# Grouping the softmax-maximum and value matmuls of two attention steps

## The chip, the core and the metric

The kernel runs on one core of a Trainium2 chip. A core has a matrix engine (TensorE: PE in the profile, its weight loads PEld), VectorE (DVE), ScalarE (ACT), GpSimd (POOL) and SyncE (SP, which here only issues DMAs). Each engine works through its own queue of instructions, and semaphores tie the queues together. The results of TensorE land in PSUM, which this kernel treats as eight banks of 128x512 f32 values; VectorE and ScalarE read them from there. The metric is device time of one execution in microseconds, lower being better.

## The reference, cut to what matters

Two times over, an attention block and a gated block are applied to `x` (2048 tokens, width 448), with the same weights in both rounds:

```python
x = x + attention(layernorm(x))      # 16 query heads of 28, one shared key and value head
x = x + glu(layernorm(x))            # (sigmoid(x Wg) * (x Wu)) Wd, inner width 1792
# attention:
scores = einsum("bhqd,bkd->bhqk", q, k) * Dh ** -0.5
o = einsum("bhqk,bkd->bhqd", softmax(scores), v)      # then @ wo
```

The softmax needs the maximum of each query's scores over all 2048 keys before the exponentials can be formed.

## The kernel before, in words

**Tiles.** A layer (l = 0, 1) is one attention block and one gated block. The 2048 queries are cut into 16 units of 128 (u = 0..15), the keys into 16 tiles of 128 (kt = 0..15), and the 16 heads into 4 groups of 4, so that one matmul has 4 heads x 128 queries = 512 columns. One step is one pair (u, kt), and a layer has 256 steps.

**What a step issues** is written out as a string, `ORDER = "FSFSFSFSPXM"` (L901), read letter by letter in the loop at L922:

- `S`, four times: `scores` (L507). One matmul (L510, tile `s`, a PSUM bank) and the exponential on ScalarE (L513), which writes the probabilities `P` in f32, from a pool of 8 tiles.
- `P`: `pv` (L516), the values of the *previous* step. Four products 128x512, each of them two matmuls, in four column strips of 32 (L521, tile `pv`, a PSUM bank of its own for the whole unit). At the end of a unit ScalarE copies them out (L525, `pvs`).
- `M`: one turn of the generator `mx_gen` (L464), which works for the *next* unit. A turn is four matmuls in four row strips of 32 (L480, tile `mx`, four banks) of one group of heads with 512 keys, and four VectorE reductions of a whole bank each (L484, `mp`). Sixteen turns make a unit. Then two small VectorE operations give the maxima `m16` (L493, L494), and `fin` (L496) transposes them on TensorE (L499, `mt`), copies them out (L501, `mr`) and sends them by a DMA from GpSimd's queue (L502) into row 28 of the query tile `QS`, from which `scores` of that unit subtracts them. `fin` waits in the list `late` for `LT = 1` turns. In unit 0 two steps take an extra turn (`MORE`), so the maxima run three turns ahead of the units.
- `X`: `tick` (L536) starts what is due of the units already finished: dividing by the sums, the output projection (`fc`, L606, twelve matmuls `wo` in one go), layer norm, transposes by DMA, and in layer 0 the keys and values of the next layer (`kv`). It also sets `rate`, the nanoseconds of filler per step: what is left, divided by the steps to go.
- `F`, four times: `Filler.slice` (L767). It first calls `flush`, which issues the deferred evictions that are due, and then lets the filler generators issue matmuls up to a quarter of `rate`, by costs written into the kernel (110 ns for a matmul of 256 columns, 190 for 448). What `tick` issued counts as debt: slices issue nothing until it is paid.

**The filler** is mostly the gated block of two finished units (`bulk`, L651): for each of 7 pairs of inner tiles a chain of 22 matmuls into `gp`, another into `up` (L345), the tanh on ScalarE (L665), the product on VectorE (L673, which frees `up`), and `parts`: a ScalarE scaling (L676) two slices after that and a VectorE remainder (L677) one slice later, into a tile `h` (pool of 10, `HB`). Then 2 x 42 matmuls `dn` (L702). The pool of `h` also holds the first tiles of `x` at the start (`load_x0`, L792). In each layer the first block of filler of this kind appears when unit 3 begins; before that the filler is query projections (`qp`).

**Banks.** One bank is kept for `pv`. The other seven are one pool, from which `s`, `mx`, `gp`, `up`, `dn`, `wo` and all other results take theirs in the written order; a matmul that has been given a bank waits until its last reader is done.

Of the kernel before, what the change touches and what calls it, by code (L numbers as in the profile page):

```python
# [19 lines left out]
def interleaved_layers_kernel(ctx: ExitStack, tc: tile.TileContext, x, wq, wk, wv, wo, wg, wu, wd, out, layers=2):  # L20
# [9 lines left out]
    H, Dh = 16, 28  # L30
    NT, NB, G, KT, FC = S // 128, S // 512, H // 4, S // 128, F // 128
    U = NT
    TB, WB, HB = 2, 4, 10
    NBL = NT // TB
    EPS = 1e-5

# [29 lines left out]
    def defer(fn, lag=0):  # L66

        pend.append((now[0] + lag, fn))
# [87 lines left out]
    def prep_q():  # L156
        parts = wk1.tile([128, 4], F32, name="parts", bufs=1)
        for c in range(4):
            junk = wk1.tile([128, D], F32, tag="P", name="junq", bufs=8)
            squares(parts[:, c:c + 1], rq[:, c], junk)  # L160
        nc.vector.tensor_reduce(mxa[:, 2:3], parts, axis=AX.X, op=OP.add)
        nc.vector.memset(WQ[:, :, :, :, Dh:32], 0.0)
        yield
        yield from scales(mxa[:, 2:3], 1, pwa[:, 2:3], swa[:, 2:3])
        for c in range(4):
            r = rq[:, c].rearrange("p (h d) -> p h d", d=Dh)
            split(WQ[:, 0, c, :, 0:Dh], WQ[:, 1, c, :, 0:Dh], r, swa[:, 2:3])
            yield
        nc.vector.tensor_scalar(esc, pwa[:, 2:3], pwa[:, 0:1], None, op0=OP.mult)
        nc.vector.tensor_scalar(esc, esc, Dh ** -0.5 * 2.0 ** -14, None, op0=OP.mult)  # L170
# [258 lines left out]
    QS, QH, PVS = {}, {}, {}  # L429
    late = []  # L430
    stored = set()
    LT = 1

    def load_qs(l, u):
        b, t = divmod(u, 4)
# [28 lines left out]
    def mx_gen(l):  # L464

        load_qh(l, 0)
        for u in range(U):
            qh = QH[l, u]
            mp = wk1.tile([128, 4, 4, NB], F32, name="mp", bufs=2)
            for kb in range(NB):  # L470
                for g in range(G):
                    for i in range(len(late) - 1, -1, -1):
                        late[i][0] -= 1
                        if late[i][0] <= 0:
                            late.pop(i)[1]()
                    assert KVD[l] >= 4 * (kb + 1)
                    ps = [psf.tile([128, 512], F32, tag=BANKS["m"], name="mx", bufs=NBK[BANKS["m"]])
                          for _ in range(4)]
                    for h in range(4):
                        nc.tensor.matmul(ps[h], qh[32 * h:32 * h + 32, g],  # L480
                                         KK[l][32 * h:32 * h + 32, 1, kb * 512:(kb + 1) * 512], start=True,
                                         stop=True, tile_position=(32 * h, 0))
                    for h in range(4):
                        nc.vector.tensor_reduce(mp[:, g, h, kb:kb + 1], ps[h], axis=AX.X, op=OP.max)  # L484
                    ps = None
                    if kb == NB - 1 and g == 2 and u + 1 < U:
                        load_qh(l, u + 1)
                    if kb * 4 + g == 7:
                        load_qs(l, u)
                    yield  # L490
            m32 = wk1.tile([128, 16], F32, name="m32")
            m16 = wk1.tile([128, 16], F16, name="m16")
            nc.vector.tensor_reduce(m32, mp.rearrange("p g h k -> p (g h) k"), axis=AX.X, op=OP.max)  # L493
            nc.vector.tensor_scalar(m16, m32, -(2.0 ** -15), None, op0=OP.mult)  # L494

            def fin(u=u, m16=m16):  # L496
                stored.add(("m", l, u))
                p = fps([16, 128], F16, "mt")
                nc.tensor.transpose(p, m16, id16)  # L499
                r = wk1.tile([16, 128], F16, name="mr")  # L500
                nc.vector.tensor_copy(r, p)  # L501
                nc.gpsimd.dma_start(QS[l, u][28:29].rearrange("o g h n -> o (g h) n"), r)  # L502
            late.append([LT, fin])
        while late:
            late.pop(0)[1]()

    def scores(l, u, kt, g, P):  # L507
        assert ("m", l, u) in stored, (l, u, kt)
        s = psf.tile([128, 512], F32, tag=BANKS["s"], name="s", bufs=NBK[BANKS["s"]])
        nc.tensor.matmul(s, KK[l][0:96, 0, kt * 128:(kt + 1) * 128], QS[l, u][:, g].rearrange("p h n -> p (h n)"),  # L510
                         start=True, stop=True)
        p = wk1.tile([128, 512], F32, tag="P", name="P", bufs=8)
        nc.scalar.activation(p, s, AF.Exp, scale=esc)  # L513
        P.append(p)

# [32 lines left out]
    class Block:  # L548
# [8 lines left out]
        def tile(self, u):  # L557
# [39 lines left out]
                yield  # L597

            def fb():
                oT = v["oT"] = wk1.tile([128, 2, 512], F16, name="oT")  # L600
                nc.scalar.copy(oT[:, 0], v["lb"])
                defer(lambda: nc.vector.tensor_tensor(oT[:, 1], v["lb"], oT[:, 0], op=OP.subtract))  # L602
                return
                yield
# [46 lines left out]
        def bulk(self):  # L651
            l, b, XT2 = self.l, self.b, self.XT2
            hs = []

            def glu(f):

                for j in range(2):
                    if f + j + 2 < FC:
                        self.load_w(f + j + 2)
                w = [self.wt.pop(f + j) for j in range(2)]  # L660
                gp = fps([128, 2, TB * 128], F32, "gp")
                for j in range(2):
                    yield from chain(gp[:, j], lambda a, c, k: w[j][:k, 0, a, c], lambda c, k: XT2[:k, c], C256, True)
                th = wk1.tile([128, 512], F32, tag="s2", name="th", bufs=3)
                defer(lambda: nc.scalar.activation(th, gp.rearrange("p j n -> p (j n)"), AF.Tanh, scale=gsc))  # L665
                up = fps([128, 2, TB * 128], F32, "up")
                for j in range(2):
                    yield from chain(up[:, j], lambda a, c, k: w[j][:k, 1, a, c], lambda c, k: XT2[:k, c], C256, True)
                h = wk1.tile([128, 2, 512], F16, name="h", bufs=HB)

                def ev():
                    t = th
                    nc.vector.scalar_tensor_tensor(t, th, 1.0, up.rearrange("p j n -> p (j n)"), op0=OP.add, op1=OP.mult)  # L673

                    def parts():
                        nc.scalar.activation(h[:, 0], t, AF.Copy, scale=2.0 ** -17)  # L676
                        defer(lambda: nc.vector.scalar_tensor_tensor(h[:, 1], t, 2.0 ** -17, h[:, 0], op0=OP.mult,  # L677
                                                                     op1=OP.subtract), 1)
                    defer(parts, 2)
                defer(ev)  # L680
                hs.append(h)

            for f in range(0, FC, 2):
                yield from glu(f)

            if not self.last and b % 2 == 0:
                XTQ[l + 1, b // 2] = big.tile([128, 7, 512], F16, tag="big", name="XT1")
            need(2 + FC)
            for t in range(TB):
                yield from self.down(t, hs)  # L690
# [207 lines left out]
        nmx += 1  # L898

    early[0] = False  # L900
    ORDER = "FSFSFSFSPXM"  # L901
    MORE = (5, 10)
    FIRST = KT * TB + 16
    KEEP = 28000
# [1 line left out]
    for l in range(layers):  # L906
# [10 lines left out]
        while late:  # L917
            late.pop(0)[1]()
        fill.slice(QCH)
        prevP = None  # L920
        rate = 0.0
        for step in range(U * KT):  # L922
            u, kt = divmod(step, KT)
            P = []
            for o in ORDER:
                if o == "S":
                    scores(l, u, kt, len(P), P)
                elif o == "M":
                    for _ in range(1 + (u == 0 and kt in MORE)):
                        next(mx, None)  # L930
                elif o == "P":
                    if prevP is not None:
                        pv(*prevP)
                elif o == "X":
                    if u and kt == 1:
                        b = (u - 1) // TB
                        if (l, b) not in BLK:
                            BLK[l, b] = Block(l, b)
                        later(*BLK[l, b].tile(u - 1))
                    if l == 0:  # L940
                        paced(step)
                    tick()
                    fed = sum(BLK[l, b].fed == TB for b in range(NBL) if (l, b) in BLK)
                    if fed < NBL - 1:
                        rate = fill.left / max(FIRST + TB * KT * fed - step, 1)
                    else:
                        rate = max(fill.left - KEEP, 0) / (U * KT - step)
                else:
                    fill.slice(rate / ORDER.count("F"))
            prevP = (l, u, kt, P)  # L950
        pv(*prevP)
        flush(True)
        later(*BLK[l, NBL - 1].tile(U - 1))
        if not final:
# [33 lines left out]
```

## Time and profile before

| | us |
|---|---|
| median of 3 runs | 2358.56 (2357.25 to 2362.03) |
| the profiled execution: its own time | 2358.22 |
| its span on the core | 2356.4 |
| TensorE busy | 2239.1 |
| VectorE busy | 1635.5 |
| ScalarE busy | 1559.2 |
| GpSimd busy | 336.8 |

The clock granted to TensorE was 0.985 of full speed over the span. Busy time of TensorE is that of matmul records whose ends are modelled, so the start of one matmul to the start of the next says more than the duration. In a row of the timeline, a figure in brackets is the idle time of that engine before the instruction, and behind it stands what ended it. "DVE L484 ... x4" is a run of four such instructions in a row, merged. A row of a waits view gives the waiting group, what released it, the sum in microseconds, the number of times and the longest one.

### The profile page before, as it was taken

Reading aid. Unit: us, or ns where it says so; the run is one execution under the profiler, and the core shown is the slowest. Engines: PE = TensorE matmul, PEld = TensorE weight load, DVE = VectorE, ACT = ScalarE, POOL = GpSimd, SP = SyncE. Lnnn points to the kernel's source line nnn. Section 1 sums busy time; section 2 is a strip of 40 time slices with the busy share of each in tenths; the row PEclk is TensorE's granted clock in tenths of the full one; section 3 lists DMA queues with packets and bytes.
Section 4 is the critical chain, followed back from the end, with each engine's and each line's share of the span. In section 5 each row is a group of like instructions: output and inputs, shape, how many; then the busy total and the mean of one; then the engine's idle time right before and its main releaser. Section 6 shows DMA issues by size and latency. Waiting matters only on the chain.

```text
span 2356.4 us, 41206 instructions
## 1 busy us (share of the span) xinstructions
PE 2239.1 (95%) x15736; PEld 1003.2 (43%) x15736; DVE 1635.5 (69%) x2917; ACT 1559.2 (66%) x2598; POOL 336.8 (14%) x602
## 2 busy tenths in 40 slices
PE   5888899999999999999998989999999999999999
PEld 3322243444444444444572224444444444444456
DVE  6888787777777777773358877867676777777321
ACT  5588676776667677677413777767676776767751
POOL 5203763100110110001101011000000000000010
PEclk9799999999999999999998999999999999999999
DMA  3244652323313132333342112222231313223133
GB/s 114 65 126 124 201 190 81 90 73 98 96 58 109 58 93 70 94 92 78 96 139 53 27 49 92 87 78 83 62 103 58 98 55 101 76 82 94 57 111 119
DMA packets 208071, 213.88 MB, mean 91 GB/s; under 512 B 139952, under 2 KB 168304, under 8 KB 207872
## 3 DMA queue, kind: packets, MB, share of 16 engines
q1 hardware_dynamic: 202496, 196.36, 28.5%
q0 software_dynamic: 5376, 14.87, 1.8%
q8 instruction: 123, 2.02, 0.4%
q14 instruction: 76, 0.62, 0.1%
HBM read 175.37 MB, written 23.59 MB: 84 GB/s over the span
## 4 chain that ended last, share of the span: by engine, by line
PE 51%; DVE 5%; DMA 1%; ACT 1%; issue 0%; SPq 0%; POOL 0%; ACTq 0%; DVEq 0%; POOLq 0%
PE pv L521 12%; PE s L510 10%; PE dn L702 8%; PE gp L345 7%; PE up L345 7%; DVE mp L484 4%; PE mx L480 4%; PE wo L612 2%; PE qp L345 1%; ACT P L513 0%; DMA sums<-rc 0%; DMA KK<-ktl 0%; DMA rc<-sums 0%; DMA sums<-pvs 0%; DVE st L297 0%
## 5 line engine op out<-in xcount | busy, mean ns | idle before, releaser
L513 ACT ACTIVATE P<-s,esc 128x512 f32<-128x512 f32 x2048 | 1307.8, 690 | 509.2 <-PE s L510 492.1
L484 DVE TENSOR_REDUCE mp<-mx 128x1 f32<-128x512 f32 x2048 | 1267.2, 681 | 412.2 <-PE mx L480 408.1
L510 PE MATMUL s<-QS,KK 96*128 96x512 f16 x2048 | 761.1, 381 | 52.7 <-DVE mp L484 34.8
L345 PEld LDWEIGHTS <-wgu 128*128 128x128 f16 x4928 | 458.6, 98 | 241.3 <-issue 94.5
L521 PE MATMUL pv<-P,VV 128*32 128x512 f32 x4096 | 547.3, 607 | 0.0
L345 PE MATMUL up<-XT,wgu 128*128 128x256 f16 x2464 | 375.6, 272 | 0.8 <-DVE mp L484 0.8
L345 PE MATMUL gp<-XT,wgu 128*128 128x256 f16 x2464 | 375.2, 274 | 0.2
L702 PE MATMUL dn<-WD,h 128*128 128x448 f16 x1344 | 321.7, 352 | 0.0
L510 PEld LDWEIGHTS <-KK 96*128 96x128 f16 x2048 | 194.5, 97 | 172.1 <-issue 93.0
L480 PE MATMUL mx<-KK,QH 32*128 32x512 f16 x2048 | 223.2, 392 | 20.7 <-ACT QH L402 4.8
L480 PEld LDWEIGHTS <-QH 32*128 32x128 f16 x2048 | 53.5, 91 | 396.5 <-issue 378.1
L702 PEld LDWEIGHTS <-h 128*128 128x128 f16 x1344 | 124.1, 98 | 136.6 <-issue 22.6
L521 PEld LDWEIGHTS pv<-P,VV 128*32 128x32 f32 x4096 | 80.9, 108 | 204.4 <-issue 192.6
L595 POOL TENSOR_TENSOR lb<-pvs,lb 128x512 f32<-128x512 f32 x32 | 40.5, 1265 | 800.3 <-DMA lb<-sums 679.4
L676 ACT ACTIVATE h<-th 128x512 f16<-128x512 f32 x112 | 70.2, 627 | 86.4 <-DVE th L673 86.3
L345 PE MATMUL qp<-XT,WQ 128*128 128x512 f16 x352 | 114.5, 403 | 3.8 <-DVE mp L484 2.4
L673 DVE SCALAR_TENSOR_TENSOR th<-th,up 128x512 f32<-128x512 f32 x112 | 75.8, 677 | 59.0 <-PE up L345 46.5
L303 POOL TENSOR_SCALAR rs<-mv 128x1 f32<-128x1 f32 (+2 forms) x53 | 13.6, 256 | 686.4 <-DVE mv L298 682.9
L677 DVE SCALAR_TENSOR_TENSOR h<-th,h 128x512 f16<-128x512 f32 x112 | 77.7, 693 | 46.7 <-ACT h L676 46.7
L665 ACT ACTIVATE th<-gp,gsc 128x512 f32<-128x512 f32 x112 | 76.8, 685 | 47.7 <-PE gp L345 47.7
L612 PE MATMUL wo<-WO,oT 128*128 128x448 f16 x384 | 78.4, 353 | 0.3 <-DVE oT L602 0.2
L345 PEld LDWEIGHTS <-WQ 128*128 128x128 f16 x352 | 34.2, 101 | 64.2 <-issue 41.1
(126 smaller groups left out, 834.3 us busy)
## 6 DMA issues: line engine op xcount, KB each, us to landing
wgu<-wgu_d SPq DMA_DIRECT2D x224, 512.0 KB
QS<-qd SPq DMA_DIRECT2D x384, 32.0 KB
lb<-sums SPq DMA_DIRECT2D x128, 64.0 KB
xr<-in_A_x_dram SPq DMA_DIRECT2D x32, 224.0 KB
qd<-qst POOLq DMA_DIRECT2D x28, 256.0 KB, 2.7
wgu_d<-sgu POOLq DMA_DIRECT2D x14, 512.0 KB, 3.8
QH<-qd SPq DMA_DIRECT2D x28, 128.0 KB
x2d<-x SPq DMA_DIRECT2D x16, 224.0 KB
```

The lines of the kernel that those rows point to most:

```text
L345: nc.tensor.matmul(ps, a, b, start=n == 0, stop=n == 10)
L480: nc.tensor.matmul(ps[h], qh[32 * h:32 * h + 32, g], KK[l][32 * h:32 * h + 32, 1, kb * 512:(kb + 1) * 512], start=True, stop=True, tile_po ...
L484: nc.vector.tensor_reduce(mp[:, g, h, kb:kb + 1], ps[h], axis=AX.X, op=OP.max)
L510: nc.tensor.matmul(s, KK[l][0:96, 0, kt * 128:(kt + 1) * 128], QS[l, u][:, g].rearrange("p h n -> p (h n)"), start=True, stop=True)
L513: nc.scalar.activation(p, s, AF.Exp, scale=esc)
L521: nc.tensor.matmul(v[32 * g:32 * g + 32], VV[l][:, kt], P[g], start=kt == 0, stop=kt == KT - 1, tile_position=(0, 32 * g))
L612: nc.tensor.matmul(p, v["oT"][:, a, h * 128:(h + 1) * 128], WO[:, c, h], start=n == 0, stop=n == 11)
L665: defer(lambda: nc.scalar.activation(th, gp.rearrange("p j n -> p (j n)"), AF.Tanh, scale=gsc))
L673: nc.vector.scalar_tensor_tensor(t, th, 1.0, up.rearrange("p j n -> p (j n)"), op0=OP.add, op1=OP.mult)
L676: nc.scalar.activation(h[:, 0], t, AF.Copy, scale=2.0 ** -17)
L677: defer(lambda: nc.vector.scalar_tensor_tensor(h[:, 1], t, 2.0 ** -17, h[:, 0], op0=OP.mult, op1=OP.subtract), 1)
L702: nc.tensor.matmul(p, hs[f // 2][:, a, o:o + 128], WD[:, f, c], start=n == 0, stop=n == 3 * FC - 1)
```

## The change: what it does

Steps are taken in pairs. In a pair of the new form (`FULL`) the even step issues two turns of the maxima and, between them, the values of the last two steps; the odd step issues neither. Two slices of filler stand in front of the first turn, which makes ten slices in a pair: six in the even step and four in the odd one. `X` stands at the end of both steps. The new form is taken from unit 1 on while `rate` is above 800; otherwise the pair has the form of before, twice. In the new form `LT` is 2. `flush` is called ahead of each turn. The scaling of `h` is deferred by four slices in place of two, in both forms. The pool of `P` grows from 8 tiles to 12; those of `h` and `oT` shrink, from 10 to 8 and from 2 to 1.

```diff
-    TB, WB, HB = 2, 4, 10
+    TB, WB, HB = 2, 4, 8
...
-    LT = 1
+    LT = [1]
...
-            late.append([LT, fin])
+            late.append([LT[0], fin])
...
-        p = wk1.tile([128, 512], F32, tag="P", name="P", bufs=8)
+        p = wk1.tile([128, 512], F32, tag="P", name="P", bufs=12)
...
-                oT = v["oT"] = wk1.tile([128, 2, 512], F16, name="oT")
+                oT = v["oT"] = wk1.tile([128, 2, 512], F16, name="oT", bufs=1)
...
-                    defer(parts, 2)
+                    defer(parts, 4)
...
-    ORDER = "FSFSFSFSPXM"
+    FULL = ("FSFSFFMPMFSFSX", "FSFSFSFSX")
+    POOR = ("FSFSFSFSPXM", "FSFSFSFSPXM")
+    ENOUGH = 800
...
-        prevP = None
+        pend_p = []
...
-            for o in ORDER:
+            if kt % 2 == 0:
+                pair = FULL if u and rate > ENOUGH else POOR
+                LT[0] = 2 if pair is FULL else 1
+            order = pair[kt % 2]
+            for o in order:
...
                 elif o == "M":
+                    flush()
                     for _ in range(1 + (u == 0 and kt in MORE)):
                         next(mx, None)
                 elif o == "P":
-                    if prevP is not None:
-                        pv(*prevP)
+                    while pend_p:
+                        pv(*pend_p.pop(0))
...
-                    fill.slice(rate / ORDER.count("F"))
-            prevP = (l, u, kt, P)
-        pv(*prevP)
+                    fill.slice(2 * rate / (pair[0] + pair[1]).count("F"))
+            pend_p.append((l, u, kt, P))
+        while pend_p:
+            pv(*pend_p.pop(0))
```

More of the change, by code (lines that the diff above doesn't have):

```diff
@@ L158, in prep_q @@
         for c in range(4):
-            junk = wk1.tile([128, D], F32, tag="P", name="junq", bufs=8)
+            junk = wk1.tile([128, D], F32, tag="P", name="junq", bufs=12)
             squares(parts[:, c:c + 1], rq[:, c], junk)
```

## The prediction, made before the changed kernel was run

> **What bounds the kernel now.** I read the page first: share of engines, then costliest groups.
>
> ```profile
> PE 2239.1 (95%) x15736; PEld 1003.2 (43%) x15736; DVE 1635.5 (69%) x2917; ACT 1559.2 (66%) x2598; POOL 336.8 (14%) x602
> ...
> L513 ACT ACTIVATE P<-s,esc 128x512 f32<-128x512 f32 x2048 | 1307.8, 690 | 509.2 <-PE s L510 492.1
> L484 DVE TENSOR_REDUCE mp<-mx 128x1 f32<-128x512 f32 x2048 | 1267.2, 681 | 412.2 <-PE mx L480 408.1
> ...
> L521 PE MATMUL pv<-P,VV 128*32 128x512 f32 x4096 | 547.3, 607 | 0.0
> ```
>
> TensorE is the bound, with VectorE and ScalarE at two thirds, one long operation each per `mx` and per `s`. But 95% is a mean over modelled ends. The windows view of two units late in layer 0, and two in layer 1 (128 score matmuls, 32 steps each), gives real lengths; the lines view of the second stretch gives what TensorE does there (`gp` has as many as `up`).
>
> ```profile
> 827.50:960.70 133.20, 48.36 (x128) 12.23 (x128) 1.00 0.29 83
> 1957.10:2088.00 130.90, 48.33 (x128) 12.22 (x128) 1.00 0.28 80
> ```
> ```profile
> L345 PE MATMUL up<-XT,wgu 128*128 128x256 f16 x154 | 24.8, 272 | 0.0
> ...
> L702 PE MATMUL dn<-WD,h 128*128 128x448 f16 x84 | 21.5, 352 | 0.0
> L612 PE MATMUL wo<-WO,oT 128*128 128x448 f16 x24 | 4.9, 353 | 0.0
> ```
>
> Then the timeline of layer 1, where starts can be read against starts.
>
> ```profile
> 1961.99 1.28 ACT L513 ACTIVATE P<-s,esc 128x512 f32<-128x512 f32 x2 [1.34 <-PE s L510]
> ...
> 1963.38 0.38 PE L510 MATMUL s<-QS,KK 96*128 96x512 f16 x1
> 1963.69 1.06 PE L521 MATMUL pv<-P,VV 128*32 128x512 f32 x8
> ...
> 1964.68 0.40 PE L480 MATMUL mx<-KK,QH 32*128 32x512 f16 x4
> 1965.01 0.50 PE L345 MATMUL up<-XT,wgu 128*128 128x256 f16 x3
> 1965.11 2.48 DVE L484 TENSOR_REDUCE mp<-mx 128x1 f32<-128x512 f32 x4 [1.35 <-PE mx L480]
> 1965.35 0.38 PE L510 MATMUL s<-QS,KK 96*128 96x512 f16 x1
> 1965.57 0.60 PE L345 MATMUL up<-XT,wgu 128*128 128x256 f16 x4
> 1966.01 0.38 PE L510 MATMUL s<-QS,KK 96*128 96x512 f16 x1
> ...
> 1967.52 1.06 PE L521 MATMUL pv<-P,VV 128*32 128x512 f32 x8
> ```
>
> A step lasts 3.83 us (1963.69 to 1967.52). A score matmul takes 0.22 to the next start, a filler matmul of 256 columns 0.11. But the score matmul *ahead of the values* takes 0.31: 0.09 extra. The values take 0.99 to 1.00 to the maxima; the page's `pv` row has 607 ns for one, so in a run of 1.06 the second four start 0.45 in, two rounds are 0.90, and 0.09 is extra. The four maxima start together and take 0.33, where one matmul as wide takes 0.22: 0.11 extra, of which I count 0.10. So each change between whole array, column strips and row strips costs TensorE about 0.1, three times a step.
>
> Per two units this makes: scores 128 x 0.22 = 28.2, values 32 x 1.09 = 34.9, maxima 32 x 0.33 = 10.6, filler 308 x 0.11 + 84 x 0.19 = 49.9 (0.19 from the `wo` row below), output projection 2 x 2.37 = 4.7. Sum 128.3. Against the lengths above, stalls are 2.6 us in layer 1 and, with what `kv` takes, 4.9 in layer 0. TensorE is nearly full, and the switches (0.28 x 32 = 9 us) are the largest thing in it that computes nothing.
>
> Where are the stalls? Mostly after the output projection:
>
> ```profile
> 1992.14 2.44 PE L612 MATMUL wo<-WO,oT 128*128 128x448 f16 x12
> 1994.51 0.39 PE L480 MATMUL mx<-KK,QH 32*128 32x512 f16 x4
> 1994.84 0.39 PE L510 MATMUL s<-QS,KK 96*128 96x512 f16 x1
> 1994.93 2.48 DVE L484 TENSOR_REDUCE mp<-mx 128x1 f32<-128x512 f32 x4 [3.73 <-PE mx L480]
> 1995.27 0.69 ACT L513 ACTIVATE P<-s,esc 128x512 f32<-128x512 f32 x1 [3.27 <-PE s L510]
> 1995.68 0.38 PE L510 MATMUL s<-QS,KK 96*128 96x512 f16 x1 [0.45 <-DVE mp L484]
> ...
> 1996.28 0.59 PE L510 MATMUL s<-QS,KK 96*128 96x512 f16 x2 [0.22 <-DVE mp L484]
> ...
> 1997.34 0.67 DVE L617 SCALAR_TENSOR_TENSOR x<-wo,osc,xr 128x448 f32<-128x448 f32 x1
> ...
> 1998.81 2.45 DVE L484 TENSOR_REDUCE mp<-mx 128x1 f32<-128x512 f32 x4
> ```
>
> Slices owe 2.37 us and issue nothing, so scores follow each other until the banks are gone: the next waits for the first reduction (1994.93 + 0.68), the third for the second. The fourth starts 0.21 later, *before* the third reduction ends (1996.8): it took the bank that ScalarE had read by 1995.96. So banks aren't handed out in strict turn; what counts is how many are open. The `wo` row also gives 0.19 per matmul and 0.10 for whole array to maxima (2.37 = 12 x 0.19 + 0.10).
>
> The waits view, over 291 to 1093 us and 1447 to 2218:
>
> ```profile
> PE s L510 <- DVE mp L484: 13.2, 33, 0.9
> PE mt L499 <- DVE m L494: 2.8, 6, 1.2
> ...
> PE s L510 <- DVE mp L484: 8.1, 24, 0.5
> ...
> ACT h L676 <- DVE th L673: 14.1, 18, 1.0
> ```
>
> **The change, part by part.** *Where it acts.* Until unit 3 the filler is query projections, here in units 1 and 2 of layer 1:
>
> ```profile
> L345 PE MATMUL qp<-XT,WQ 128*128 128x512 f16 x43 | 16.2, 382 | 1.0 <-DVE mp L484 1.0
> ```
>
> 43 x 216 (the kernel's cost) / 32 steps = 290, under 800: form of before. With a gated block, 49,840 / 32 = 1557: new form. That is 95 pairs per layer (unit 3 from kt = 2 to unit 14), and 8 in unit 15, whose maxima are done: 190 and 16.
>
> *Switches.* A pair now has six: two each of 0.09, 0.09, 0.10. The new order has four: filler to maxima 0.10, maxima to values (not in the trace), values to maxima 0.09, maxima to filler 0.10. For the unseen one the nearest rows are the other three, 0.09 to 0.10; its bounds are 0, if strips to strips need nothing, and 0.20, if it pays both ways. I take 0.10. Saved: 0.56 - 0.39 = 0.17 to 0.18 per pair, 190 x 0.177 = 33.6 us (15 to 53 by the bounds). The Trainium skill, TensorEngine Tiling (Array Packing), section Key Properties, says that a change of tiling mode drains TensorE; by it strips to strips is a fourth drain, as I took it, and 0 is out. In unit 15 two of 0.09 go per pair: 16 x 0.18 = 2.9. `wo` and `kv` leave the place between values and maxima for the end of a step, among whole-array work: about 24 x 0.10 = 2.3.
>
> *Transposes a turn later.* TensorE no longer waits for `m16`: 2.8 us of layer 0 go (0 to 2.8). Late next is row 28 of `QS`: `mt` now stands at kt = 14, 5.8 us ahead of the next unit's first score.
>
> ```profile
> L502 POOL DMA_DIRECT2D QS<-mr x32 | 19.0, 594 | 170.0 <-DVE mr L501 167.0 <-DVE mp L484 2.4 <-DMA XT<-hl 0.5
> ...
> QS<-mr POOLq DMA_DIRECT2D x32, 4.0 KB, 2.5
> ```
>
> Transpose and copy 0.6, issue 0.6, landing 2.5: 3.7. 2.1 us to spare on GpSimd's queue; I cost it at 0. If one group of reductions (2.48) stood ahead of the copy, it would be 0.4 per unit, 9 us in all.
>
> The turns also issue SP's twelve loads of `QS` at kt = 4 and the load of `QH` at kt = 10, as now, used a unit and a pair and a half later: 0.
>
> *Pools.* Ten `P` are open when the values begin, twelve before the first is freed: 12 suffice. A block holds 7 `h`, so 8 suffice; `oT` is read 14 steps before it is written again. At the start 8 tiles of `x` are under way in place of 10; the closest is tile 11, whose buffer comes free at 24.9 and which is read at 28.36:
>
> ```profile
> 3.28 0.63 DVE L816 BATCH_NORM_STATS2 st<-xr 128x6 f32<-128x448 f32 x1 [1.03 <-DMA xr<-in_A_x_dram]
> ...
> 28.36 0.61 DVE L816 BATCH_NORM_STATS2 st<-xr 128x6 f32<-128x448 f32 x1
> ```
> ```profile
> 23.98 0.92 POOL L316 TENSOR_TENSOR hl<-xr,hl 128x384 f16<-128x384 f32 x1
> ```
>
> The first load, issued at 0.7, was there at 3.3; 3.4 are left: 0, at most 2 us if SP's queue adds to it.
>
> *Stalls, the disputed term.* Two turns put eight reductions in a row on VectorE. Timetable of a pair with 0.31 per slice (49.9 / 160): first maxima at 1.78, values 2.11, second maxima 4.01, scores at 4.65, 5.18, 5.71, 6.24, 6.77, 7.30, end 7.52. Reductions start 0.43 after the maxima and 0.60 apart, so banks come free at 2.89, 3.49, 4.09, 4.69, 5.29, 5.89, 6.49, 7.09. At 4.01 the second turn takes the last four of seven: two still hold first maxima, one the filler. The next score has one at 4.09, the one after at 4.69; then ScalarE returns banks too (first at 5.8). No wait, with 0.4 to 0.5 to spare. ScalarE, at 0.60 against 0.53 per score, ends the last exponential at 8.8, 0.5 before the next maxima want four banks. A score that waits holds up all of TensorE behind it; a `th` that waits behind reductions holds up ScalarE's `h` and every exponential after it. What eats these margins is a filler's operation of 0.6 to 0.7 at the wrong place: a tanh or an `h` among six exponentials (about every second gated pair, 0.2 over), a VectorE one just ahead of the first turn, an `up` that waits behind eight reductions. I take 0.2 per gated pair (bounds 0 and 0.4), 0.05 per `dn` pair. After `wo` the pair has no filler up to its second score of the odd step, and `x` with its statistics (1997.34 to 1998.81, 1.5 us) now runs ahead of the reductions: the reductions free banks at 2.6, 3.2, 3.9, 4.5, 5.0 after it, and the third score behind the second maxima starts at 5.0 in place of 3.75, so 1.25 is lost (now 1.0). `parts` two slices later lets `th` finish first, so ScalarE loses fewer waits:
>
> ```profile
> 1971.34 0.68 DVE L673 SCALAR_TENSOR_TENSOR th<-th,up 128x512 f32<-128x512 f32 x1
> ...
> 1972.05 0.63 ACT L676 ACTIVATE h<-th 128x512 f16<-128x512 f32 x1 [1.05 <-DVE th L673]
> ```
>
> That is in the 0.2. Per two units: 2 x 1.25 + 11 x 0.2 + 3 x 0.05 = 4.9 where 2.6 is now; I take the same 2.3 more in layer 0. Given back: 2.3 x 12 = 27 us.
>
> *Sum* against the profiled execution's 2358.2 (median of the runs 0.3 above): -33.6 - 2.9 - 2.3 - 2.8 + 27 = -15; 2343.
>
> **The rivals.** *A, full gain.* Stalls stay as they are: -42, 2317. For it: timetable without a wait, the 14.1 us of ScalarE waits gone. Against: margins of half a microsecond where one operation takes 0.7.
>
> *B, evacuation binds: slower.* If banks come in the planned turn after all, each change between `gp` and `up` in the five slices behind the second maxima shifts every later score to the next reduction, and at 6.77 it waits for 7.09, or later: 0.4. Gated pairs have 1.3 such changes in ten slices, 0.64 in those five: 0.26. With 0.1 each from ScalarE and VectorE that is 0.45 a pair, and after `wo`, where all six scores then wait in turn, 1.9: 11 x 0.45 + 3.8 + 0.2 = 9.0 per two units, 6.4 x 12 = 77 given back: 2393; if half of the waits overlap, 2370. It decides from 0.33 per gated pair on. For it: above, two of three scores waited for reductions in turn. Against: the third. The Trainium skill, TensorEngine Tiling (Array Packing), section PSUM Bottleneck, speaks for B: packing speeds TensorE, not the emptying of PSUM, which may become the bound; the trace so far gives it no more than the chance below.
>
> *C, QS late:* +9 on the forecast, 2352. *D, new form not taken*, `rate` under 800: 2358.
>
> **How the numbers follow.** Forecast (2325 to 2353) 0.40, A 0.17, B 0.33, C or balance 0.08, D 0.02. A measurement can tell about 0.2%, 4.7 us. C's 0.08 counts 0.07 as same, D's 0.02 all. Faster 0.40 + 0.17 + 0.01, same 0.09, slower 0.33. The range leaves out 0.08 of A's far end and 0.12 of B's: 2312 to 2388.
>
> **What would show it.** Right: timeline rows with maxima, sixteen `pv`, maxima; maxima to values at 0.33; 190 such places; `PE mt <- DVE m` near 0; two units of layer 1 in about 130.3. B would show as `PE s <- DVE mp` above 30 us in place of 8.1, scores starting 0.05 behind every reduction of the second group. Wrong would be maxima to values well off 0.33, or `PE s <- DMA QS` at unit starts.

## The result, and the profile after

The changed kernel takes 2396.24 us (median of 6 runs, 2392.41 to 2397.66) against 2358.89 for the kernel before (6 runs): 1.0154 times as long, 95% interval 1.0141 to 1.0167. It is slower by 37 us, well clear of the scatter of the runs. The forecast was 15 us faster, and the range ended at 2388.

From the page of the changed kernel, the rows that answer to those of before:

```profile
span 2393.0 us, 41446 instructions
...
PE 2251.8 (94%) x15736; PEld 1047.5 (44%) x15736; DVE 1638.6 (68%) x2917; ACT 1501.3 (63%) x2598; POOL 336.6 (14%) x602
...
L513 ACT ACTIVATE P<-s,esc 128x512 f32<-128x512 f32 x2048 | 1257.0, 696 | 588.1 <-PE s L510 579.4
L484 DVE TENSOR_REDUCE mp<-mx 128x1 f32<-128x512 f32 x2048 | 1256.8, 681 | 211.9 <-PE mx L480 207.5
...
L521 PE MATMUL pv<-P,VV 128*32 128x512 f32 x4096 | 510.2, 608 | 0.0
...
L480 PE MATMUL mx<-KK,QH 32*128 32x512 f16 x2048 | 271.7, 392 | 47.0 <-ACT P L513 16.9
```

The row of the maxima on the page of the kernel before:

```profile
L480 PE MATMUL mx<-KK,QH 32*128 32x512 f16 x2048 | 223.2, 392 | 20.7 <-ACT QH L402 4.8
```

TensorE has as many matmuls as before, and one `mx` still has 392 ns. What stands out is their row: busy time from 223.2 to 271.7, idle time before them from 20.7 to 47.0. The busy time of a group is the union of its records. Four matmuls of one turn that start together cover 0.39 us; when the fourth starts late they cover more. So 48.5 + 26.3, some 75 us, are turns whose matmuls start late or don't start together. The idle time alone would have shown a third of it.

The windows view, two units of 32 steps in each layer (the columns after the length are TensorE's busy time and count of score matmuls):

```profile
841.30:977.40 136.10, 48.14 (x128) 12.32 (x128) 0.99 0.28 82
```
```profile
1922.00:2054.70 132.70, 48.14 (x128) 12.32 (x128) 1.00 0.27 79
```

They were 133.2 and 130.9. Now the timeline of one pair in layer 1, TensorE and VectorE in order of time:

```profile
1619.65 0.38 PE L345 MATMUL gp<-XT,wgu 128*128 128x256 f16 x2
...
1619.96 0.40 PE L480 MATMUL mx<-KK,QH 32*128 32x512 f16 x4
1619.97 0.69 DVE L602 TENSOR_TENSOR oT<-lb,oT 128x512 f16<-128x512 f32 x1 [1.76 <-ACT oT L601]
...
1620.29 1.92 PE L521 MATMUL pv<-P,VV 128*32 128x512 f32 x16
...
1620.58 0.68 DVE L677 SCALAR_TENSOR_TENSOR h<-th,h 128x512 f16<-128x512 f32 x1
1621.18 3.07 DVE L484 TENSOR_REDUCE mp<-mx 128x1 f32<-128x512 f32 x5
1622.15 0.74 PE L480 MATMUL mx<-KK,QH 32*128 32x512 f16 x4
1622.82 0.39 PE L345 MATMUL gp<-XT,wgu 128*128 128x256 f16 x2
```

The switches cost about what was worked out. Maxima to values takes 0.33 (1619.96 to 1620.29). Two filler matmuls and the change to maxima take 0.31 (1619.65 to 1619.96), of which 0.09 is extra. Two steps of values and the switch take 1.86 (1620.29 to 1622.15). But `oT` (L602) and `h` (L677) stood ahead of the first reductions on VectorE, which began 1.22 after their maxima in place of 0.43. The second turn began at 1622.15. Its last matmul of 0.39 ends with the pack at 1622.89, so it began at 1622.5, when the second reduction of the first turn had ended (0.60 + 0.68 after 1621.18). The pack covers 0.74 in place of 0.40, and TensorE goes on at 1622.82 in place of 1622.48.

In layer 0 a longer chain holds the first turn of some pairs:

```profile
839.22 4.87 DVE L484 TENSOR_REDUCE mp<-mx 128x1 f32<-128x512 f32 x8 [1.92 <-PE mx L480]
844.01 0.67 DVE L710 SCALAR_TENSOR_TENSOR x<-dn,dsc,x 128x448 f32<-128x448 f32 x1
...
845.38 0.18 DVE L298 BATCH_NORM_AGGREGATE mv<-st 128x2 f32<-128x6 f32 x1
...
846.59 0.39 PE L480 MATMUL mx<-KK,QH 32*128 32x512 f16 x3
...
847.45 0.19 POOL L308 TENSOR_TENSOR rs<-rs 128x1 f32<-128x1 f32 x1
847.67 0.52 DVE L322 TENSOR_SCALAR xn<-x,mv,rs 128x448 f32<-128x448 f32 x1 [2.11 <-POOL rs L308]
848.22 0.56 ACT L314 CAST hl<-xn 128x448 f16<-128x448 f32 x1 [2.16 <-DVE xn L322]
848.69 1.26 ACT L513 ACTIVATE P<-s,esc 128x512 f32<-128x512 f32 x2
...
849.42 0.58 PE L480 MATMUL mx<-KK,QH 32*128 32x512 f16 x1 [2.44 <-ACT P L513]
849.93 3.18 PE L521 MATMUL pv<-P,VV 128*32 128x512 f32 x16
```

The new rows `x` and their statistics stand behind eight reductions on VectorE; the statistics are done there at 845.56, GpSimd works on them until 847.64, VectorE has been waiting for it 2.11 us, ScalarE for VectorE 2.16. Behind that copy stand the exponentials, and the bank of the first of them is what the fourth `mx` needs: three start at 846.59, the fourth 2.83 us later.

The last row shows one thing more: the sixteen `pv` behind that wait take 3.18 us in place of 1.92. The clock granted to TensorE was 0.50 from 849.1 to 852.5. In units 3 to 14 of layer 0 TensorE stands idle for 2.2 to 2.5 us inside a first turn six times (up to 296.5, 430.7, 566.0, 712.1, 849.4 and 985.5). Within 0.5 us of the end of four of these waits, from 565.8, 712.6, 849.1 and 985.6, the granted clock is 0.50 for 3.4 us; why not at the other two isn't shown. The kernel before has no wait of that length there and one such drop, at 591.1. A drop costs at most half of its 3.4 us, so three more cost at most 5 of the 17.5 us that these units lose.

Going through all late starts of units 3 to 14 in the timeline and taking what ended just ahead of each, the waits of turns add up, for layers 0 and 1, to 30.1 and 6.2 us for an exponential (first turns), 3.6 and 2.3 for a tanh (first), 4.8 and 4.8 for `x` behind the output projection (first), 11.9 and 9.2 for a reduction (second turns). That is 72.9 in all; before, it was about 1.

Where the 37 us lie, by unit lengths (start of one copy of the values at line 525 to the next): units 3 to 14 of layer 0 went from 815.7 to 833.2, those of layer 1 from 784.4 to 795.8, and the rest of the span from 756.3 to 764.0. So 29 us are lost where the new form acts, and 8 elsewhere.

### The profile page after: what moved, and what is told of

The parts are those of the page before. It is cut to its first block, busy times and chain, and to the rows that moved or that the text cites. A ratio compares the mean times of both kernels' runs of the same rounds, so it can differ in the third digit from the quotient of the medians.

```text
span 2393.0 us, 41446 instructions
## 1 busy us (share of the span) xinstructions
PE 2251.8 (94%) x15736; PEld 1047.5 (44%) x15736; DVE 1638.6 (68%) x2917; ACT 1501.3 (63%) x2598; POOL 336.6 (14%) x602
## 4 chain that ended last, share of the span: by engine, by line
PE 61%; DVE 19%; ACT 9%; issue 3%; DMA 2%; POOL 1%; SPq 1%; ACTq 0%; POOLq 0%; DVEq 0%
DVE mp L484 14%; PE s L510 14%; PE pv L521 12%; PE dn L702 10%; PE up L345 9%; PE gp L345 7%; ACT P L513 6%; PE mx L480 5%; PE wo L612 3%; PE qp L345 1%; DVE st L297 1%; DVE x L617 1%; DVE h L677 1%; ACT h L676 1%; DMA lb<-sums 1%
## 5 line engine op out<-in xcount | busy, mean ns | idle before, releaser
L513 ACT ACTIVATE P<-s,esc 128x512 f32<-128x512 f32 x2048 | 1257.0, 696 | 588.1 <-PE s L510 579.4
L345 PEld LDWEIGHTS <-wgu 128*128 128x128 f16 x4928 | 469.7, 98 | 253.7 <-issue 71.4
L521 PE MATMUL pv<-P,VV 128*32 128x512 f32 x4096 | 510.2, 608 | 0.0
L345 PE MATMUL gp<-XT,wgu 128*128 128x256 f16 x2464 | 387.6, 273 | 0.7 <-DVE mp L484 0.2
L345 PE MATMUL up<-XT,wgu 128*128 128x256 f16 x2464 | 387.6, 272 | 0.2
L702 PE MATMUL dn<-WD,h 128*128 128x448 f16 x1344 | 329.6, 352 | 0.8
L480 PE MATMUL mx<-KK,QH 32*128 32x512 f16 x2048 | 271.7, 392 | 47.0 <-ACT P L513 16.9
L510 PEld LDWEIGHTS <-KK 96*128 96x128 f16 x2048 | 195.9, 97 | 152.1 <-issue 64.7
L521 PEld LDWEIGHTS pv<-P,VV 128*32 128x32 f32 x4096 | 103.4, 110 | 284.8 <-issue 278.2
L677 DVE SCALAR_TENSOR_TENSOR h<-th,h 128x512 f16<-128x512 f32 x112 | 77.6, 693 | 78.4 <-ACT h L676 78.3
L617 DVE SCALAR_TENSOR_TENSOR x<-wo,osc,xr 128x448 f32<-128x448 f32 x32 | 21.9, 684 | 79.3 <-PE wo L612 79.3
```

The costliest lines, as they stand in the source:

```text
L345: nc.tensor.matmul(ps, a, b, start=n == 0, stop=n == 10)
L480: nc.tensor.matmul(ps[h], qh[32 * h:32 * h + 32, g], KK[l][32 * h:32 * h + 32, 1, kb * 512:(kb + 1) * 512], start=True, stop=True, tile_po ...
L521: nc.tensor.matmul(v[32 * g:32 * g + 32], VV[l][:, kt], P[g], start=kt == 0, stop=kt == KT - 1, tile_position=(0, 32 * g))
L702: nc.tensor.matmul(p, hs[f // 2][:, a, o:o + 128], WD[:, f, c], start=n == 0, stop=n == 3 * FC - 1)
```

## The experiments

**Theory 1**: the new order saves TensorE what was forecast, and loses more in waits for banks, since each turn takes four banks at once and VectorE and ScalarE return them late. **Theory 2**: the new order itself costs TensorE, or the loss lies in the other parts. Each run is compared with the kernel before on the same chip, 2358 to 2360 us.

### Relief for the engines that empty the banks

Reductions over half of the columns (half of the scores is left out of the maxima), exponentials over half (the values read one half twice), or both, in the changed order (pair) and in the one before (step):

```diff
-    nc.vector.tensor_reduce(mp[:, g, h, kb:kb + 1], ps[h], axis=AX.X, op=OP.max)
+    nc.vector.tensor_reduce(mp[:, g, h, kb:kb + 1], ps[h][:, 0:256], axis=AX.X, op=OP.max)
...
-    nc.scalar.activation(p, s, AF.Exp, scale=esc)
+    nc.scalar.activation(p[:, 0:256], s[:, 0:256], AF.Exp, scale=esc)
...
-    nc.tensor.matmul(v[32 * g:32 * g + 32], VV[l][:, kt], P[g], start=kt == 0, stop=kt == KT - 1,
+    nc.tensor.matmul(v[32 * g:32 * g + 32], VV[l][:, kt], P[g][:, 0:256].rearrange("p (o n) -> p o n", o=1).to_broadcast([128, 2, 256]), start=kt == 0, stop=kt == KT - 1,
```

> The changed kernel with both halved, reductions and exponentials. Theory 1: TensorE is left with its own work and four switches per pair; 30 to 42 us below the kernel of before with the same two halvings. Theory 2: above it or equal.

> The kernel of before with both halved, reductions and exponentials. The reference for the run with the new order: its stalls (2.6 us per two units in layer 1, 4.9 in layer 0) go, six switches per two steps stay; 2290 to 2320 by both theories.

Measured: 2231.68 us for the pair form (ratio to the kernel before 0.9462, 0.9435 to 0.9490) and 2264.52 for the step form (0.9602, 0.9574 to 0.9629). The pair form is 33 us faster when both engines are relieved, as theory 1 expected. Units 3 to 14 of both layers take 1527.2 us against 1567.1: 39.9 less. The step form came out below its expected 2290, since the relief also shortened the start and the time between the layers, which no term of the forecast had looked at. The rows of the maxima:

```profile
L480 PE MATMUL mx<-KK,QH 32*128 32x512 f16 x2048 | 226.5, 390 | 23.8 <-ACT P L513 8.7
```
```profile
L480 PE MATMUL mx<-KK,QH 32*128 32x512 f16 x2048 | 213.3, 388 | 18.8 <-DMA QH<-qd 4.8
```

The first is the pair form: 271.7 and 47.0 have become 226.5 and 23.8. Against the step form that is still 13.2 and 5.0 more, so turns of the pair form wait some 18 us even here, and the 40 us are what is left after that. Theory 2 falls as far as TensorE's own cost goes: in these units the order is worth 40 us or more, once banks come back sooner.

> The changed kernel with the reductions of the maxima over 256 of the 512 columns of each bank (the other half of the scores is left out of the maxima). Theory 1 (emptying the banks binds: packs of four maxima and scores wait for a bank that VectorE or ScalarE frees late): VectorE's run of eight falls from 4.9 to about 2.9 us, most waits go, 2320 to 2350. Theory 2 (the new order costs TensorE itself more, or the loss lies outside the paired steps): within 10 us of 2396.

> The changed kernel with the exponentials over 256 of the 512 columns, the values reading these columns twice (half of the scores is left out of the probabilities). If ScalarE's train of exponentials is what holds the first pack of a pair (theory 1, ScalarE's part), the waits of maxima for ScalarE, the largest kind in layer 0, go: 2345 to 2375; if VectorE's run of eight is the cause alone, within 10 us of 2396. Theory 2: within 10 us of 2396.

> The kernel of before with the reductions of the maxima over 256 of 512 columns (half of the scores is left out of the maxima), the reference for pair_half_dve (2286.6). If VectorE's run of eight is what the pair form loses by, the order of before gains less in units 3 to 14 from the same relief: these 24 units, 1600 us before, fall to 1575 to 1590, while the pair form stands at 1565; in all 2295 to 2310. If the relief helps both alike, they fall to 1540 to 1550 and the kernel to about 2260.

Halved reductions alone: 2286.56 in the pair form (0.9695, 0.9667 to 0.9723), far under the expected range, and 2282.33 in the step form (0.9675, 0.9656 to 0.9694), under it too. In units 3 to 14 the pair form gains 64 us (1629.0 to 1565.0), the step form 31 (1600.1 to 1569.5), which is more than the 10 to 25 expected and half of what the pair form gets. Of the 40 us that its order is worth there, the pair form has 4.5; first turns still wait 25.7 us for an exponential in layer 0 and 12.5 in layer 1. What VectorE alone doesn't give back is ScalarE's part: halving the exponentials as well takes another 37.8 us off these units in the pair form (1565.0 to 1527.2), and 2.4 in the step form (1569.5 to 1567.1). Halved exponentials alone give 2340.61 (0.9924, 0.9895 to 0.9953), just under the range of theory 1, and 38 us in units 3 to 14. The waits of first turns for an exponential in layer 0, which were to go, fall only from 30.1 to 22.3 there. So a good part of them isn't the length of the exponentials; they stand behind something else, which the chain above names.

### That chain

```diff
-    v["hl"] = ln_split(v["x2"], *v["ls"], eng=nc.vector, hi=nc.scalar.copy)
+    v["hl"] = ln_split(v["x2"], *v["ls"], eng=nc.vector)
```

> The changed kernel with one operation moved from ScalarE to VectorE: the f16 copy of the normalised rows in db (only in layer 0, 16 times). In the changed kernel the largest single kind of wait of a first pack of maxima, 14.7 us in nine places of layer 0, follows a chain: statistics late on GpSimd, VectorE waits for them, ScalarE waits for VectorE and holds the exponentials behind it. If ScalarE standing in line for that copy is what costs the 14.7, units 3 to 14 of layer 0 fall by 8 to 15 us and the kernel to 2382 to 2388. If the exponentials would have been late anyway, it stays within 4 us of 2396.

Measured 2384.40 (1.0103, 1.0087 to 1.0120), 12 us under the changed kernel and within the expected range. Units 3 to 14 of layer 0 take 822.3 in place of 833.2, and first turns there wait 14.8 us for exponentials in place of 30.1, while second turns wait 19.3 for reductions in place of 11.9: the wait for the statistics is now VectorE's alone, and half of what it cost moves to the other bank. As theory 1 has it. The waits of turns account for 7.9 of the 10.9 us. Five of the six waits of over 2 us are gone, and with them three of the four drops of the clock in these units, which can be the rest.

### The other parts of the change

```diff
-    ENOUGH = 800
+    ENOUGH = 10 ** 9
```

> The changed kernel with the threshold for the new form at 10^9, so that no pair has it; the other parts (flush ahead of each turn, scaling four slices later, pools) stay. By the unit lengths, 8 to 10 us of the 37 lie outside units 3 to 14 (units 1 and 2, the time between the layers). Theory: these come from the parts that act in every step: 2364 to 2372, with units 1 and 2 longer as in the changed kernel. Rival: they are an after-effect of the paired steps; then 2356 to 2361.

```diff
                 elif o == "M":
-                    flush()
```

> As poor_always, without the flush ahead of each turn. If that call costs units 1 and 2 and the time between the layers (it puts evictions that are due ahead of the four reductions on VectorE, and on ScalarE earlier), this run is 5 to 10 us below poor_always and near 2359. If the later scaling or the pools cost it, it is equal to poor_always within 3 us.

> The changed kernel without the flush ahead of each turn. In the form of before it cost 11.7 us (poor_always to poor_no_flush), by the order of VectorE's queue after the output projection. In the paired form the projection stands at the end of a step and a slice flushes ahead of the turn anyway: theory, only the steps in the old form gain, 3 to 6 us, 2390 to 2393. Rival: the flush also hurts in paired steps, 8 us or more: under 2388.

Without any pair in the new form the kernel takes 2364.11 (1.0018, 1.0008 to 1.0027), with units 1 and 2 at 58.0 and 64.7 (changed kernel 58.1 and 65.4; before 56.6 and 63.1): the low end of what the theory gave. Without the flush as well it takes 2352.41 (0.9971, 0.9960 to 0.9983): the flush costs 11.7, a little more than expected, and the rest of the parts gain 6. What the flush does shows in VectorE's waits of poor_always, between 291 and 1093 us:

```profile
DVE x L617 <- PE wo L612: 40.2, 12, 3.6
```

In the kernel of before it isn't among the first nine of that list. The twelve matmuls of the output projection stand between values and maxima; the flush behind them puts their eviction ahead of the four reductions in VectorE's queue, and VectorE stands 3.4 us each time until the projection is done. How that reaches TensorE isn't shown: its listed waits in the same stretch add up to 17.9 us in poor_always (8.9 of scores for reductions, 6.0 for exponentials) and 17.2 in poor_no_flush (13.3 and 0.2). In the paired form the flush costs about 6: 2390.38 (1.0132, 1.0117 to 1.0147), as expected for steps in the old form alone; 4.3 us of it lie outside units 3 to 14.

```diff
-                    defer(parts, 2)
+                    defer(parts, 4)
```

> The kernel of before with one edit: the scaling of h four slices later in place of two. poor_no_flush, which also has the other pools, is 6.3 us below the kernel of before, and ScalarE's waits for th fall there from 18.0 us to 1.7 in layer 0. If the later scaling is the whole of it: 2351 to 2355. If the pools have a part (8 tiles at the start): above 2356.

The kernel of before with this edit alone: 2353.30 (0.9975, 0.9965 to 0.9984), so the later scaling is nearly the whole gain of 6, and the pools cost nothing that can be told in the form of before. With the paired form they were not tried alone. ScalarE's waits between 291 and 1090 us in this run:

```profile
ACT h L676 <- DVE th L673: 1.7, 1, 1.7
```

and in the kernel of before:

```profile
ACT h L676 <- DVE th L673: 18.0, 20, 1.6
```

### Turns apart

```diff
-    FULL = ("FSFSFFMPMFSFSX", "FSFSFSFSX")
+    FULL = ("FSFSFMPFSFSX", "FSFSMFSFSX")        # pair_split
```

> The changed kernel with the two turns of a pair apart: even step FSFSFMPFSFSX, odd step FSFSMFSFSX. Values of two steps still go together behind one turn; the other turn stands alone half a pair later, so VectorE has four reductions at a time, not eight; five switches per pair, one fewer than before. Theory 1 (the run of eight costs what the switches save): 12 to 25 us are saved against the order of before and the waits of maxima for banks fall below 10 us a layer; 2340 to 2362 with what the other parts cost. Theory 2 (the values of two steps together, or the trains of scores on ScalarE, cost it): 2380 or more.

> pair_split without the flush ahead of each turn. If the flush costs only the steps in the old form: 2348 to 2351. If it costs the turns of the split form too: 2338 to 2345.

pair_split takes 2353.87 (0.9976, 0.9967 to 0.9986): with the run of eight split the loss is gone though the values of two steps still go together, so theory 2's version of it falls too. The waits of turns did not fall below 10 us a layer, though: for exponentials alone they are 22.9 and 8.0, the scores being right in front of each turn. Without the flush it takes 2347.37 (0.9952, 0.9937 to 0.9966), just under the first case of its expectation: it points to a flush that costs the old form's steps only.

```diff
+    FULL = ("FSFSFPMFSFSX", "FSFSFMFSFSX")       # split_values_first, no flush
```

> Two turns apart and no flush, but the values of two steps stand ahead of the first turn and a slice of filler ahead of the second: even step FSFSFPMFSFSX, odd step FSFSFMFSFSX. In pair_split the packs still wait 23 us for ScalarE's exponentials in layer 0 and 8 in layer 1, since scores stand right in front of them. If that is what is left, 1.9 us of values in front of one pack and a slice in front of the other take most of it away: 10 us or more under split_no_flush, 2330 to 2342. If VectorE is what is left (turns 2.9 and 4.6 us apart): equal to split_no_flush or above.

This took the waits of turns away, as its row shows, but not the time: 2347.05 (0.9946, 0.9932 to 0.9961), equal to split_no_flush.

```profile
L480 PE MATMUL mx<-KK,QH 32*128 32x512 f16 x2048 | 239.5, 391 | 21.3 <-ACT QH L402 4.8
```

The row of split_no_flush has 266.2 and 32.2. Units 3 to 14 of layer 0 are 9.0 shorter than there, those of layer 1 are 7.0 longer. In layer 1 (1460 to 2212) scores now wait 9.6 us for reductions, up to 1.5 at a time, where split_no_flush lists none: the wait moved from turns to scores, behind turns that stand 2.95 us apart. The time between the layers is 3.0 longer as well, and why wasn't tried.

> split_values_first with the f16 copy of the normalised rows on VectorE, the edit that took 12 us off the paired form. If the copy only hurts where eight reductions make the statistics late, nothing is gained: within 3 us of 2347. If it also holds the exponentials here, 2340 to 2344.

2342.57 (0.9934, 0.9919 to 0.9949): the fastest order found that computes everything, 16 us under the kernel before. The copy seems to cost something in this order too: 4.5 us by the medians, 2.9 by the ratios to the kernel before on the same chip, 3.0 in units 3 to 14 of layer 0. The two intervals overlap, so this isn't shown; it is at most about a third of the 12 there.

### Between the layers

```diff
-    pair = FULL if u and rate > ENOUGH else POOR
+    pair = FULL if 0 < u < U - 1 and rate > ENOUGH else POOR
```

> The changed kernel with unit 15 in the form of before. The time from the end of unit 15 of layer 0 to the end of unit 0 of layer 1 is 4.2 us longer in the changed kernel. If unit 15 in the paired form leaves its last values and filler for that time: it falls back by 3 to 4 us, and the two units 15 are 0.8 and 1.0 longer; 2393 to 2395. If it is not an after-effect of unit 15: 2396 to 2399.

Measured 2392.14 (1.0145, 1.0125 to 1.0166), two runs, just under the expected range and below the lowest of the changed kernel's six (2392.41) only in one of them. From the end of unit 15 of layer 0 to the end of unit 0 of layer 1 it takes 181.8 us in place of 185.3 (before: 181.1), and the units 15 are 0.9 and 1.1 longer. That fits an after-effect of unit 15 in the paired form, nearly twice its gain of 2.0, but doesn't show it: step_scale_later has no paired step and takes 184.1 for the same stretch. TensorE's waits of the changed kernel in that time (1165 to 1351 us) have one that isn't in the same list of pair_not_unit15:

```profile
PE s L510 <- DMA QS<-mr: 2.0, 1, 2.0
```

It is 2.0 of the 3.5 us; the rest was not found.

## Why the prediction was wrong

- **Switches: right in kind, and somewhat too small.** Maxima to values was taken as 0.10 extra, and is (0.33 against 0.22). That this is the switch and not the pack itself shows where two packs follow each other: in the changed kernel at 134.74, 1311.52 and 1329.28 the second begins 0.23 behind the first, at a granted clock of 1.00. The Trainium skill's rule that a change of tiling mode drains TensorE (TensorEngine Tiling (Array Packing), Key Properties) holds for strips to strips too, by that 0.10. Values to maxima was under-sized: 1.86 for two steps and 1.00 for one leave 0.43 for a round and 0.14 for the switch, where 0.45 and 0.09 had been taken. In a pair, two changes from scores to values and one from values to maxima go, and one from filler to maxima comes: 2 x 0.09 + 0.14 - 0.09 = 0.23 saved, and 190 pairs make 43 us in place of 33.6; all 190 are in the timeline. With the banks relieved, units 3 to 14 gain 39.9 us, and the terms for them (33.6 + 2.3 + 2.8) give 38.7. That agreement is in part luck, since the 39.9 have some 18 us of waits of turns in them and whatever the step form still waits.
- **Unit 15:** 2.9 forecast, 1.8 gained in the units themselves, and perhaps 3.5 lost just behind the first of them, which was not foreseen.
- **Transposes a turn later: mostly not gained.** In units 3 to 14 `PE mt` waits 1.2 in layer 0 in place of 2.8, and 1.2 in layer 1, where it had not waited: 0.4 gained of the 2.8. Both are the last transposes of a layer, which `mx_gen` issues at once when it ends (1096.9 and 2238.5); all the others of these units are in time, as forecast. Row 28 of `QS` is late once, between the layers. TensorE's waits in the changed kernel, first from 291 to 1110 us and then from 1460 to 2250:

```profile
PE mx L480 <- ACT P L513: 16.4, 12, 2.5
PE s L510 <- DVE mp L484: 4.3, 19, 0.3
PE mx L480 <- DVE mp L484: 3.7, 14, 0.8
PE mt L499 <- DVE m L494: 1.2, 1, 1.2
```
```profile
PE s L510 <- DVE mp L484: 9.9, 36, 0.3
PE mx L480 <- DVE mp L484: 1.4, 6, 0.2
PE mt L499 <- DVE m L494: 1.2, 1, 1.2
```

- **The step that failed is the disputed term**, "No wait, with 0.4 to 0.5 to spare" and "I take 0.2 per gated pair", 27 us given back. Units 3 to 14 lost 28.9 although the order saves about 43 there, so some 72 were given back, 0.38 a pair more than before's stalls; the waits of turns listed above are 72.9 against about 1. The timetable looked at the right moment, "the second turn takes the last four of seven", but it was made for engines on time, and the addition for late ones was made with scores in mind. A score needs one bank and can take whichever comes next. A turn needs four, so it waits for the slowest of four, and TensorE's whole queue with it. In the rows above scores of layer 0 wait *less* than before, 4.3 against 13.2 (in layer 1 it is 9.9 against 8.1), and the turns, which hardly waited before, have taken their place. These rows show only what left TensorE idle; most of the 72.9 lies inside packs that count as busy.
- **A second part of that step:** in-order chains across engines. Eight reductions don't only return their own banks late; what stands behind them on VectorE is late for GpSimd and ScalarE, and the exponentials behind those hold banks too. For these waits layer 0 was given nothing of its own ("I take the same 2.3 more"); moving the copy alone takes back 11 of its 17.5 us, the clock's part included, which the prediction didn't look at.
- **Costed in one place only: the flush ahead of each turn.** The prediction has `x` ahead of the reductions behind the output projection of a pair, and nothing for steps in the old form. The flush costs 11.7 us with all steps in the old form and about 6 in the changed kernel. The later scaling was folded into the 0.2; alone it gains 5. Pools: 0, as said, where that was tried.
- **Rival B** (2393) had the size and the cause, banks emptied too slowly. Its place was wrong: it put the waits on scores and named `PE s <- DVE mp` above 30 us in layer 1 as its mark, which came out at 9.9. So its number was right by luck. Its second figure doesn't follow either: half of its 77 is 38, which gives 2355 and not 2370. Its page rule, that packing speeds TensorE and not the emptying of PSUM (the Trainium skill, TensorEngine Tiling (Array Packing), PSUM Bottleneck), is what the runs with halved reductions and exponentials bear out: 33 us faster than the order of before with both relieved, 37 slower without.

## What to carry to other kernels

Before grouping matmuls that each need a bank, count for every group the *last* bank it needs and who returns it, with that engine late by one operation of its other work; a group of four waits for the slowest of four, and everything behind it waits too. When switches between array shapes are worth saving, group those whose results stay in one bank (the values here) and keep those that fill many banks apart: with the turns apart the kernel took 2347 us, with the turns together 2390, and with the order of before 2352, all other parts the same. (The step from 2352 to 2347 is at the edge of the scatter, the one from 2390 is far beyond it.) Judge waits of packed matmuls by the busy time of their group as well as by its idle time, since a pack with one late member counts as busy.

## What the runs showed that was not expected

VectorE is busy 69% of the span and TensorE 95%, and yet halving the reductions takes 76 us (3.2%) off the kernel of before. 47 of them lie outside units 3 to 14: 17.6 up to the end of unit 0 of layer 0, 13.2 between the layers, 10.9 in units 1 and 2 of layer 1. These stretches have little or no filler, and the shorter reductions show there at once: VectorE sets much of their pace.
